# Three stages in one kernel: weights of the first expert issued together, zero stores at unit 14, a later fill tile and two tiles of tokens split early

## Chip, cores and metric

The kernel runs on one core of a Trainium2 chip. The time is device microseconds of one execution; several executions are timed and the median is given. The profile is one execution, recorded by the hardware.

## What is computed

The reference chains three stages over 1,152 tokens (2 batches of 576) of width 512, in float32.

```python
scores = scale * np.matmul(q, k.transpose(0, 1, 3, 2))      # 8 heads of 64
scores = np.where(masks, scores, -1000000000.0)             # 4 heads: last 32 keys; 4 heads: every 32nd key
x = softmax(scores) @ v                                     # -> (1152, 512)
logits = x @ w_gate + modality_bias[modality_id]            # 8 experts
e_idx = np.argmax(logits, axis=1)
out[e_idx == e] = gate_w * (np.maximum(x @ w1[e], 0) @ w2[e])   # one expert a token; w1 512x1024, w2 1024x512
# second layer: 4 experts, every token through all of them
out += p[:, e:e+1] * (np.maximum(x @ w1[e], 0) @ w2[e])
```

## The kernel before

**Attention** (first 66 us). The masked attention is cut into 20 units of 128 rows (`units`, `NU` = 20): six strided ones and five local ones for the first batch (units 0 to 10), then five strided and four local ones. A software pipeline over `s` runs `scores(s)`, `transp(s-2)`, `norm(s, s-4)`, `pv(s-3)` and `xtr(s-5)`. `norm` also stores the unit's result rows to the scratch `xe` in HBM (lines 378 and 383) from the SyncE queue (SP): one store for a local unit, two for a strided one. Every DMA of SP takes the next of eight semaphores in turn and waits until the one that had it before has landed.

**Routing and the fill tile.** The gate's logits of the first batch give the most frequent expert while the second batch is still in attention (`route0`). Up to 128 of its tokens become the *fill tile*: `first_tile` gathers their rows from `xe` (line 596), and the generator `plain_tile` (lines 609 to 653), kept as `fill`, computes them in plain float32 between other work. Its steps: one with four transposes (line 617), eight with a first-layer matmul each (line 623; the profile shows a float32 matmul as two), one with eight transposes (line 636), four with second-layer matmuls (line 643), then the scaling and the store (lines 652, 653). `early(n)` runs it up to step n; the list `EF` gives n for the last units, for the place after `logits_part(1, 0)`, after the first step of `logits(1)`, and after the rest. The expert's eight weight blocks of 512 KB go to `raws[0..7]`: two in `route0` (`W1A` = 2), the others from unit 20 on (`W1S`), two and then one for each later `s`, between the row stores of units 17 to 19. Five stores of zeros to rows of `ye` that no tile writes (line 736) are issued at `s == NU - 1`.

After the second batch's logits, `ranks` and a chain of small VectorE operations (lines 778 to 843) place every token in one of 11 tiles of 128 by expert (`idx16`). Two gathers (line 852) fetch the rows of tiles 0 and 1; the four-matmul transposes of tile 0 (line 860) stand between the fill tile's second-layer steps 12 and 13. A conditional block for more tiles (line 911) follows; it is skipped here.

**First expert layer** (`moe1`, to about 235 us). The float32 operands are split into a high part, cast by ScalarE (line 846), and a low part, subtracted by VectorE (line 847), and each product takes three matmuls. `Weights.ahead(most)` splits blocks in the order of their use while fewer than `most` are held; a block whose expert is the one of the tile before is not loaded again (a skipped DMA). `moe1` runs `mm1` of tile k (four blocks) between the transposes of the hidden rows of tile k-1 (`htr`, line 1032), then `mm2` of tile k-1 (lines 1046 to 1048). `xprep(k)` gathers the gate weights of tile k, transposes and splits its tokens (`x_parts`) and issues the gather of tile k+2. The PSUM pool `ps_a` of these transposes has two banks; a bank is free when VectorE has taken the low part from it. All engines run their own instructions in program order.

**Second expert layer** (from about 235 us) is not touched.

Of the kernel before, what the change touches and what calls it, by code (L numbers as in the profile page):

```python
# [28 lines left out]
KC = DM // P  # L29
FC = FF // P  # L30
# [81 lines left out]
def fused_kernel(  # L112
# [37 lines left out]
    RING, RAW = 10, 8  # L150
# [10 lines left out]
    def load_block(raw, src, cond=None):  # L161
        nc.sync.dma_start(out=raw.rearrange("p (c f) -> p c f", c=src.shape[1]), in_=src, cond=cond)
# [134 lines left out]
    NU = len(units)  # L297
# [88 lines left out]
    def transp(u):  # L386
        kind, i = units[u]
        w = KW if kind == 0 else GQ
        pt = ps2.tile([P, 512], F32, name="ps_t")[:, : 2 * P].rearrange("p (a b) -> p a b", a=2)
        for pr in range(2):  # L390
            nc.tensor.transpose(
                pt[: 2 * w, pr], st[u][:, 2 * pr : 2 * pr + 2].rearrange("p h k -> p (h k)"), ident
            )
        pts = a3.tile([P, 2, P], F32, name="pts")
        nc.scalar.copy(pts[: 2 * w], pt[: 2 * w])
        st[u] = pts
# [271 lines left out]
    def route0():  # L668
        logits_part(0, 1)
        logits_part(0, 0)  # L670
        yield from logits(0)
        rk = ranks(0)
        fav = favourite(rk[:, TPB])
        for _ in range(4):
            next(fav)
        eg.append(expert_value(gtab[0:1, 0:1]))
        for c in range(W1A):
            load_block(raws[c], w1_block(eg[0], c))
        yield
        for n, _ in enumerate(turns(lanes(0, rk), fav)):  # L680
            if n % 2:
                yield
        yield from first_tile()
# [20 lines left out]
            filled += 1  # L704


    W1A, W1S = 2, 20
    nw = W1A
    r0 = route0()
    EF = 0, 0, 1, 1, 1, 2, 4  # L710
    for s in range(NU + 5):
        if s == 9:
            ax.close()
            gp = ctx.enter_context(tc.tile_pool(reuse_waits="tile", name="gp", bufs=5, side="right"))
            xctx = ctx.enter_context(ExitStack())
            xp = xctx.enter_context(tc.tile_pool(reuse_waits="tile", name="xp", bufs=2, side="right"))
            ectx = ctx.enter_context(ExitStack())
            ep = ectx.enter_context(tc.tile_pool(reuse_waits="tile", name="ep", bufs=1, side="right"))
            ge = gp.tile([P, XW], F32, name="g")
            ye0 = xp.tile([P, XW], F32, name="ye0", bufs=1)  # L720
            zero = ep.tile([P, FF], F32, name="he")
            nc.gpsimd.memset(zero[:, :XW], 0.0)
        if s < NU:
            scores(s)
        if 0 <= s - 2 < NU:
            transp(s - 2)
        norm(s, s - 4)
        if 0 <= s - 3 < NU:
            pv(s - 3)
        if 0 <= s - 5 < NU:  # L730
            xtr(s - 5)
        if s == 12:
            late_setup()
        if s == NU - 1:
            for t in range(NST + 1, NSX + 1):
                nc.sync.dma_start(out=ye[t * P : (t + 1) * P, :], in_=zero[:, :XW])
        if s - 5 >= nb0 - 1:
            next(r0, None)
            if s >= R2:
                next(r0, None)  # L740
        if s == NU:
            for _ in r0:
                pass
            logits_part(1, 1)
        if s >= W1S and W1A <= nw < FC:
            for _ in range(2 if s==W1S else 1):
                load_block(raws[nw], w1_block(eg[0], nw) if nw < KC else w2_block(eg[0], nw - KC))
                nw += 1
        if s > NU:
            early(EF[s - NU - 1])  # L750
    while nw < FC:
        load_block(raws[nw], w2_block(eg[0], nw - KC))
        nw += 1
    logits_part(1, 0)
    early(EF[4])
    lg = logits(B - 1)
    next(lg)
    early(EF[5])
    for _ in lg:
        pass  # L760
    early(EF[6])
    rk = ranks(B - 1)
# [100 lines left out]
    def x_parts(g, pt=None):  # L863
        pt = pt or x_transposed(g)
        xh = xp.tile([P, 512], F32R, name="xh")
        xl = xp.tile([P, 512], F32R, name="xl")
        split(xh, xl, pt)
        return xh, xl

    gs = {k: m1_gather(k, gp) for k in range(2)}  # L870
    for n in range(5):
        if n == 3:
            x0 = x_transposed(gs[0])
# [131 lines left out]
    def moe1(mp, tiles, W, gs, pool, mid, after, before_last):  # L1005
        n = len(tiles)
        xs, hs, ys = {}, {}, {}

        def xprep(k):
            g = gs.pop(k)  # L1010
            y = mp.tile([P, XW], F32, name="y", bufs=3)
            with_rows(y, idx16[:, tiles[k] : tiles[k] + 1])
            xs[k] = x_parts(g) if k else x0
            ys[k] = y
            if k + 2 < n:
                gs[k + 2] = m1_gather(tiles[k + 2], pool)

        def mm1(k, ph, kc):
            xh, xl = xs[k]
            key = "1", tiles[k], kc  # L1020
            wh, wl = W.out.pop(key)
            s = slice(P * kc, P * (kc + 1))
            for xx, ww, first, last in ((xh, wh, kc == 0, False), (xh, wl, False, False), (xl, wh, False, kc == KC - 1)):
                for i in range(2):
                    nc.tensor.matmul(ph[i], xx[:, s], ww[:, 512 * i : 512 * (i + 1)], start=first, stop=last)  # L1025
            W.release(key)

        def htr(k, i, ht):
            pt = pst.tile([P, 512], F32, name="ps_a")
            for c in range(4):  # L1030
                s = slice(512 * i + P * c, 512 * i + P * (c + 1))
                nc.tensor.transpose(pt[:, P * c : P * (c + 1)], hs[k][:, s], ident)  # L1032
            hh = mp.tile([P, 512], F32R, name="hh")
            hl = mp.tile([P, 512], F32R, name="hl")
            split(hh, hl, pt)
            ht.append((hh, hl))

        def mm2(k, ht, py, u):
            key = "2", tiles[k], u
            wh, wl = W.out.pop(key)  # L1040
            for i in range(2):
                kc = 2 * u + i
                hh, hl = ht[kc // 4]
                s = slice(P * (kc % 4), P * (kc % 4 + 1))
                f = slice(512 * i, 512 * (i + 1))
                nc.tensor.matmul(py, hh[:, s], wh[:, f], start=(kc == 0), stop=False)  # L1046
                nc.tensor.matmul(py, hh[:, s], wl[:, f], start=False, stop=False)  # L1047
                nc.tensor.matmul(py, hl[:, s], wh[:, f], start=False, stop=(kc == FC - 1))  # L1048
            W.release(key)

        xprep(0)
        xprep(1)
        W.ahead()
        for k in range(n + 1):
            ht = []
            if k == n:
                before_last(W, 0)
            if k < n:
                ph = [psb.tile([P, 512], F32, name="ps_b") for _ in range(2)]
                mm1(k, ph, 0)  # L1060
            if k > 0:
                htr(k - 1, 0, ht)
            W.ahead()
            if k == n:
                before_last(W, 1)
            if k < n:
                mm1(k, ph, 1)
            if k > 0:
                htr(k - 1, 1, ht)
            W.ahead()  # L1070
            if k < n:
                mm1(k, ph, 2)
                if 0 < k < n - 1:
                    xprep(k + 1)
                W.ahead()
                mm1(k, ph, 3)
                h = mp.tile([P, FF], F32, name="h")
                for i in range(2):
                    nc.scalar.activation(h[:, 512 * i : 512 * (i + 1)], ph[i], AF.Relu)
                hs[k] = h  # L1080
                W.ahead()
            if k > 0:
                py = psb.tile([P, 512], F32, name="ps_b")
                for u in range(4):
                    mm2(k - 1, ht, py, u)
                    if k == n and u < 3:
                        before_last(W, 2 + u)
                    mid(tiles[k - 1], u)
                    if u < 3:
                        W.ahead()  # L1090
                y = ys.pop(k - 1)
                nc.scalar.activation(y[:, :DM], py, AF.Copy, scale=y[:, DM : DM + 1])  # L1092
                t = tiles[k - 1]
                nc.scalar.dma_start(out=ye[(t + 1) * P : (t + 2) * P, :], in_=y)
                W.ahead()
                after(t)
# [275 lines left out]
    places2 = [[(m2b[n][1], len(m1b) + n) for n in (2 * u, 2 * u + 1)] for u in range(NU2)]  # L1372
    W = Weights(m1b + m2b, raws, len(m1b))
    PC = Pieces()
    W.ahead(3)
    x0 = x_parts(gs[0], x0)
    W.ahead(4)
    for _ in fill:
        pass
    W.owner[KC:] = [None] * (RAW - KC)  # L1380
    W.load()
    W.ahead()
    ectx.close()
    x2p = ctx.enter_context(tc.tile_pool(reuse_waits="tile", name="x2p", bufs=1))
    xh2, xl2 = (x2p.tile([P, 7, 2, HP * CHT[0]], F32R, name=n) for n in ("xh2", "xl2"))
# [211 lines left out]
```

## Time and profile before

| what | value |
|---|---|
| median of 3 runs | 631.07 us (630.07 to 634.13) |
| profiled execution | 631.46 us |
| its span on the core | 629.7 us |
| mean granted TensorE clock | 0.987 |
| TensorE (PE) matmuls, busy | 596.2 us (95% of the span) |
| VectorE, ScalarE, GpSimd busy | 417.2, 350.7, 249.5 us |
| DMA | 79.14 MB, mean 126 GB/s |

Busy times of engines overlap. PEld is TensorE's weight loads, which run beside matmuls. A granted clock of 1.00 is 2.4 GHz and 0.50 is 1.2 GHz. Times in the rows are microseconds from the span's start; in a group's row the mean is in nanoseconds. An idle time in square brackets is that of the engine just before the instruction, with what ended it.

### The profile page before, as it was taken

Reading aid. Unit: us, or ns where it says so; the run is one execution under the profiler, and the core shown is the slowest. Engines: PE = TensorE matmul, PEld = TensorE weight load, DVE = VectorE, ACT = ScalarE, POOL = GpSimd, SP = SyncE. Lnnn points to the kernel's source line nnn. Section 1 sums busy time; section 2 is a strip of 40 time slices with the busy share of each in tenths; the row PEclk is TensorE's granted clock in tenths of the full one; section 3 lists DMA queues with packets and bytes.
Section 4 is the critical chain, followed back from the end, with each engine's and each line's share of the span. In section 5 each row is a group of like instructions: output and inputs, shape, how many; then the busy total and the mean of one; then the engine's idle time right before and its main releaser. Section 6 shows DMA issues by size and latency. Waiting matters only on the chain.

```text
span 629.7 us, 10388 instructions
## 1 busy us (share of the span) xinstructions
PE 596.2 (95%) x3620; PEld 498.8 (79%) x3620; DVE 417.2 (66%) x738; ACT 350.7 (56%) x690; POOL 249.5 (40%) x309
## 2 busy tenths in 40 slices
PE   4897798999999989999999999999999999999995
PEld 3554446888877878888988889898889988999984
DVE  3467369999896875668677677575565567557541
ACT  2354169888988874555656555554444544444420
POOL 9312023113696444275657656332342112312203
PEclk9999799999998999999999999999999999999999
DMA  8983951543479764353223231322421223121002
GB/s 189 200 187 109 315 161 47 168 143 94 144 229 316 231 222 150 122 165 101 101 92 110 72 129 68 135 84 88 144 87 67 69 74 124 71 68 68 0 2 84
DMA packets 35346, 79.14 MB, mean 126 GB/s; under 512 B 6520, under 2 KB 9856, under 8 KB 34904
## 3 DMA queue, kind: packets, MB, share of 16 engines
q1 hardware_dynamic: 30632, 67.08, 33.8%
q0 software_dynamic: 2784, 7.95, 4.1%
q10 hardware_dynamic: 1872, 3.39, 1.4%
q8 instruction: 30, 0.49, 0.3%
q14 instruction: 28, 0.23, 0.1%
HBM read 98.49 MB, written 9.28 MB: 171 GB/s over the span
## 4 chain that ended last, share of the span: by engine, by line
PE 77%; ACT 2%; DVE 2%; issue 2%; DMA 2%; POOL 1%; SPq 0%; POOLq 0%; DVEq 0%; ACTq 0%
PE ps_b L1269 9%; PE ps_b L1270 9%; PE ps_b L1271 9%; PE ps_b L1025 8%; PE ps_b L1418 7%; PE ps_b L1417 7%; PE ps_b L1420 7%; PE ps_a L1417 3%; PE ps_a L1418 3%; PE ps_a L1420 3%; PE ps_b L1048 3%; PE ps_b L1047 2%; PE ps_b L1046 2%; PE ps_a L1032 1%; ACT wh L846 1%
## 5 line engine op out<-in xcount | busy, mean ns | idle before, releaser
L1189 DVE TENSOR_TENSOR wl<-raw,wh 128x512 fp32r<-128x512 f32 (+1 forms) x160 | 125.6, 786 | 51.7 <-ACT wh L1188 51.0
L847 DVE TENSOR_TENSOR wl<-raw,wh 128x1024 fp32r<-128x1024 f32 x88 | 107.5, 1252 | 20.0 <-ACT wh L846 19.6
L1188 ACT CAST wh<-raw 128x512 fp32r<-128x512 f32 (+1 forms) x160 | 102.9, 664 | 3.5 <-POOL raw L1212 3.3
L1209 POOL TENSOR_TENSOR raw<-raw 128x256 f32<-128x256 f32 x32 | 24.1, 753 | 200.1 <-DVE wl L1189 200.1
L846 ACT CAST wh<-raw 128x1024 fp32r<-128x1024 f32 x88 | 90.1, 1055 | 8.6 <-ACT y L1092 3.6
L1281 DVE TENSOR_TENSOR m2t<-ps_b,raw 128x320 f32<-128x320 f32 (+1 forms) x93 | 42.1, 453 | 40.3 <-PE ps_b L1271 39.2
L1269 PE MATMUL ps_b<-xh,wh 128*128 128x256 f32 x224 | 63.8, 285 | 1.0 <-DVE xh L1281 0.5
L1271 PE MATMUL ps_b<-xh,wl 128*128 128x256 f32 x224 | 63.0, 281 | 0.0
L1270 PE MATMUL ps_b<-xl,wh 128*128 128x256 f32 x224 | 63.0, 281 | 0.0
L1269 PE MATMUL ps_b<-x,wh 128*128 128x320 f32 x160 | 49.6, 310 | 0.0
L1270 PE MATMUL ps_b<-x,wh 128*128 128x320 f32 x160 | 49.4, 309 | 0.0
L1271 PE MATMUL ps_b<-x,wl 128*128 128x320 f32 x160 | 49.4, 309 | 0.0
L1269 PEld LDWEIGHTS ps_b<-xh,wh 128*128 128x128 f32 x224 | 42.2, 189 | 7.1 <-ACT raw L1302 0.9
L1270 PEld LDWEIGHTS ps_b<-xl,wh 128*128 128x128 f32 x224 | 42.2, 188 | 4.2
L1284 ACT ACTIVATE hh2b<-m2t 128x256 fp32r<-128x256 f32 (+1 forms) x45 | 20.0, 443 | 44.3 <-DVE m2t L1281 41.0
L1284 ACT ACTIVATE hh2a<-m2t 128x256 fp32r<-128x256 f32 (+1 forms) x42 | 18.7, 445 | 44.5 <-DVE m2t L1281 44.5
L1271 PEld LDWEIGHTS ps_b<-xh,wl 128*128 128x128 f32 x224 | 42.3, 189 | 0.0
L605 POOL DMA_INDIRECT y<-xx,idx x11 | 12.9, 1177 | 60.4 <-DMA ye<-y 41.3
L1046 PE MATMUL ps_b<-wh,hh 128*128 128x512 f32 x88 | 35.1, 399 | 1.5 <-ACT hh L846 1.5
L1417 PE MATMUL ps_b<-wh,hh2a 128*128 128x512 f32 x90 | 35.5, 395 | 0.0
L1418 PE MATMUL ps_b<-wl,hh2a 128*128 128x512 f32 x90 | 35.5, 395 | 0.0
L1417 PE MATMUL ps_b<-wh,hh2b 128*128 128x512 f32 x90 | 35.5, 394 | 0.0
(274 smaller groups left out, 1546.0 us busy)
## 6 DMA issues: line engine op xcount, KB each, us to landing
raw<-in_w1a_dram SPq DMA_DIRECT2D x48, 512.0 KB
raw<-in_w2a_dram SPq DMA_DIRECT2D x48, 512.0 KB
raw<-in_w1b_dram SPq DMA_DIRECT2D x32, 512.0 KB
raw<-in_w2b_dram SPq DMA_DIRECT2D x32, 512.0 KB
ye<-y ACTq DMA_DIRECT2D x11, 260.0 KB
kvl<-in_kvl_dram SPq DMA_DIRECT2D x2, 792.0 KB
ye<-he SPq DMA_DIRECT2D x5, 260.0 KB
kvl<-in_kvl_dram SPq DMA_DIRECT2D x2, 614.0 KB
```

Of the source, the lines that this page charges most:

```text
L846: nc.scalar.copy(dst_h, src)
L847: nc.vector.tensor_tensor(dst_l, src, dst_h.bitcast(F32), op=ALU.subtract)
L1025: nc.tensor.matmul(ph[i], xx[:, s], ww[:, 512 * i : 512 * (i + 1)], start=first, stop=last)
L1046: nc.tensor.matmul(py, hh[:, s], wh[:, f], start=(kc == 0), stop=False)
L1188: return (lambda: nc.scalar.copy(h[:, s], src[:, s])), (lambda: nc.vector.tensor_tensor(l[:, s], src[:, s], h[:, s].bitcast(F32), op=ALU.s ...
L1189: lambda: nc.vector.tensor_tensor(l[:, s], src[:, s], h[:, s].bitcast(F32), op=ALU.subtract)
L1269: nc.tensor.matmul(ph, wh[:, kc], xh, start=first and kc == 0, stop=False, skip_group_check=True)
L1270: nc.tensor.matmul(ph, wh[:, kc], xl, start=False, stop=False, skip_group_check=True)
L1271: nc.tensor.matmul(ph, wl[:, kc], xh, start=False, stop=kc == 1, skip_group_check=True)
L1417: nc.tensor.matmul(po, hh, wh, start=(fb == 0 and fh == 1), stop=False, skip_group_check=part)
L1418: nc.tensor.matmul(po, hh, wl, start=False, stop=False, skip_group_check=part)
L1420: nc.tensor.matmul(po, hl, wh, start=False, stop=last, skip_group_check=part)
```

## The change

The edits are of order only; no instruction computes anything else. `W1A` becomes 1 and the other seven weight blocks are all issued at `s == 20`, ahead of the stores of units 17, 18 and 19. The zero stores move from `s == 19` to `s == 14` (`ZS`), right behind the store of unit 10. `EF` drops all of the fill tile's steps from the loop: its transposes come behind the first step of `logits(1)` instead of ahead of the last `xtr` and of `logits_part(1, 0)`, and its later steps move back by one. Before `moe1`, tile 0's tokens are split after two blocks instead of three, tile 1's tokens are transposed and split after five blocks (before: in `xprep(1)`, after ten), and nine blocks instead of ten are split ahead. In `moe1` the calls of `W.ahead` during tile 0 fall away but for the one behind its `Relu`, which then splits five blocks.

```diff
-    W1A, W1S = 2, 20
+    W1A, W1S, ZS = 1, 20, 14
...
-    EF = 0, 0, 1, 1, 1, 2, 4
+    EF = 0, 0, 0, 0, 0, 1, 3
...
-        if s == NU - 1:
+        if s == ZS:
             for t in range(NST + 1, NSX + 1):
                 nc.sync.dma_start(out=ye[t * P : (t + 1) * P, :], in_=zero[:, :XW])
...
         if s >= W1S and W1A <= nw < FC:
-            for _ in range(2 if s==W1S else 1):
+            while nw < FC:
                 load_block(raws[nw], w1_block(eg[0], nw) if nw < KC else w2_block(eg[0], nw - KC))
                 nw += 1
...
-            xs[k] = x_parts(g) if k else x0
+            xs[k] = x_parts(g) if k > 1 else x01[k]
...
         xprep(0)
         xprep(1)
-        W.ahead()
         for k in range(n + 1):
...
             if k > 0:
                 htr(k - 1, 0, ht)
-            W.ahead()
+                W.ahead()
...
             if k > 0:
                 htr(k - 1, 1, ht)
-            W.ahead()
+                W.ahead()
             if k < n:
                 mm1(k, ph, 2)
                 if 0 < k < n - 1:
                     xprep(k + 1)
-                W.ahead()
+                if k:
+                    W.ahead()
                 mm1(k, ph, 3)
...
-    W.ahead(3)
-    x0 = x_parts(gs[0], x0)
-    W.ahead(4)
+    W.ahead(2)
+    x01 = [x_parts(gs[0], x0)]
+    W.ahead(KC + 1)
+    x01.append(x_parts(gs[1]))
+    W.ahead(KC + 2)
     for _ in fill:
         pass
     W.owner[KC:] = [None] * (RAW - KC)
     W.load()
-    W.ahead()
+    W.ahead(RING - 1)
```

## Rows read from the trace of the kernel before

**Rows 1.** The page: busy time by engine, share of the span, instructions.
```profile
PE 596.2 (95%) x3620; PEld 498.8 (79%) x3620; DVE 417.2 (66%) x738; ACT 350.7 (56%) x690; POOL 249.5 (40%) x309
```

**Rows 2.** Busy time by stretch: engines, then granted clock, DMA share, GB/s.
```profile
60.00:70.00 10.00, 5.43 (x67) 3.65 (x66) 3.92 (x19) 2.19 (x7) 2.73 (x3) 0.89 0.73 237
70.00:80.00 10.00, 10.00 (x43) 4.49 (x42) 4.89 (x36) 1.42 (x4) 0.00 (x0) 0.77 0.96 335
...
90.00:100.00 10.00, 7.69 (x33) 5.50 (x32) 9.86 (x10) 9.59 (x12) 7.40 (x6) 1.00 0.28 84
...
110.00:120.00 10.00, 10.00 (x52) 8.21 (x51) 9.28 (x10) 8.73 (x12) 2.18 (x2) 1.00 0.42 131
...
80.00:81.00 1.00, 1.00 (x3) 0.29 (x2) 0.93 (x5) 0.60 (x1) 0.00 (x0) 1.00 1.08 413
```

**Rows 3.** Timeline of TensorE: start, duration, line, operation, tiles, count, idle before.
```profile
68.86 1.12 PE L617 MATMUL ps_t<-mk,g 128*128 128x128 f32 x4 [2.76 <-DMA g<-xe,idxe]
...
82.66 3.70 PE L643 MATMUL ps_a<-raw,hte 128*128 128x512 f32 x8
86.19 0.60 PE L860 MATMUL ps_a<-mk,g 128*128 128x128 f32 x4
86.63 3.60 PE L643 MATMUL ps_a<-raw,hte 128*128 128x512 f32 x8
91.53 0.66 PE L860 MATMUL ps_a<-mk,g 128*128 128x128 f32 x4 [1.30 <-DVE xl L847]
```

**Rows 4.** Timeline of the SyncE queue, issue of the zero stores and weights.
```profile
56.06 4.43 SPq L383 DMA_DIRECT2D xe<-raw  x6
...
66.20 3.93 SPq L736 DMA_DIRECT2D ye<-he  x5
70.23 0.77 SPq L378 DMA_DIRECT2D xe<-rw  x1
71.22 1.13 SPq L162 DMA_DIRECT2D raw<-in_w1a_dram  x2
...
74.79 0.42 SPq L378 DMA_DIRECT2D xe<-rw  x1
```

**Rows 5.** Line 852 from 79 to 84 us: its instructions in ns, first and last start.
```profile
L852 POOLq EVENT_SEMAPHORE  x4: 17/43/1659, 79.3 to 81.1; - x4
...
DMA to landing us min/median/max: 3.4/3.5/3.6
```

**Rows 6.** Timeline at the start of the first expert layer: ScalarE, VectorE, TensorE's next wait.
```profile
86.30 2.94 ACT L846 CAST wh<-raw 128x1024 fp32r<-128x1024 f32 x3 [3.13 <-SPq L911]
...
91.39 8.26 DVE L847 TENSOR_TENSOR wl<-raw,wh 128x1024 fp32r<-128x1024 f32 x7
...
91.67 5.79 ACT L846 CAST wh<-raw 128x1024 fp32r<-128x1024 f32 x6 [0.41 <-ACT ye L652]
...
100.69 1.08 ACT L1079 ACTIVATE h<-ps_b 128x512 f32<-128x512 f32 x2
...
104.71 0.68 DVE L847 TENSOR_TENSOR hl<-ps_a,hh 128x512 fp32r<-128x512 f32 x1
...
105.45 0.66 PE L860 MATMUL ps_a<-mk,g 128*128 128x128 f32 x4 [0.22 <-DVE hl L847]
```

**Rows 7.** The chain that ended last, pieces of TensorE: start, duration.
```profile
92.19 5.62 PE ps_b L1025 x24
...
106.11 1.39 PE ps_b L1025 x6
...
114.40 0.44 PE ps_a L1032 x4
```

**Rows 8.** TensorE after its wait at 187 us, and stretches around both waits.
```profile
189.68 0.66 PE L1136 MATMUL ps_b<-mk,g 128*128 128x128 f32 x4 [2.29 <-DMA g<-ye,cidx]
...
69.00:74.00 5.00, 5.00 (x20) 2.48 (x21) 0.00 (x0) 1.17 (x3) 0.00 (x0) 0.50 0.90 308
...
190.00:194.00 4.00, 4.00 (x14) 3.18 (x12) 1.33 (x1) 3.14 (x7) 3.36 (x7) 0.58 1.03 358
```

## The prediction

> **What bounds the kernel now.** The page comes first: TensorE is busy for 95% of the span [rows 1]. The stretches then show where it is not the bound: from 110 us on it is busy throughout, but between 60 and 70 us it works little more than half the time, and between 90 and 100 us three quarters [rows 2]. All edits lie between 56 and 106 us, so only there can time be won, and what TensorE has won when it stops waiting is kept.
>
> The timeline of TensorE names its waits [rows 3]. At 68.86 it has stood 2.76 us for the rows of the fill tile, at 91.53 it has stood 1.30 us for VectorE. In the five microseconds after the first wait the granted clock is 0.50, that is 1.2 GHz [rows 8]. The five zero stores take 3.93 us of SyncE's queue just ahead of most weight blocks [rows 4]. ScalarE starts the splits of the first expert layer at 86.30, released by SyncE after 3.13 us of waiting, and from there VectorE sets the pace: TensorE's transposes of tile 2's tokens, at 105.45, wait for its `hl` [rows 6]. The start of these transposes is where I measure the gain; TensorE's next long wait, at 187 us, is of another kind [rows 8].
>
> **The fill tile's place.** Gone is the wait of 2.76 us, and the 1.2 GHz of 69 to 74 us if TensorE keeps working: five microseconds at half rate held 2.5 us of work [rows 3, 8]. One step of two matmuls, 3.70 / 4 = 0.9 us by those of line 643 [rows 3], moves from ahead of `ranks` to behind it. That would be 6 us; I take 5 as the lead of the routing chain, since the transposes of the fill tile still stand ahead of the logits'. Behind `ranks` come six steps instead of five, 0.9 us longer, and they need weight block 1 (below), which I let cost 0.6: line 643 starts 3.5 us earlier, at 79.2, and its first half ends at 79.2 + 3.7 = 82.9.
>
> **The zero stores.** Issued behind unit 10's store, they precede the six stores that begin at 56.06. Their price on SyncE moves with them: at most the 3.93 us of before, at least 5 x 0.42 = 2.1 us, the duration of the store at 74.79 [rows 4]. I take 2.6, nearer to the lower end, as fewer transfers are queued there. Behind them wait the stores of units 11 to 13, the gate weights' store, block 0 and the stores of units 14 and 15, later by 2.6 us until block 1, no longer issued there, gives back about 0.7. None of these ends a wait: the fill tile's rows are of units 0 to 10, and block 0 has the fill tile's transposes ahead of its first use. At 66.20 their 1.3 MB are out of the way.
>
> **The weights.** Unit 16's store goes out near 68.0 in place of 70.23. Blocks 1 to 7 follow every 0.75 us from 68.6 to 73.2: between the 0.57 of the pair at 71.22 and the 0.99 from the store to it [rows 4]. For a block with nothing ahead of it I take 3.7 us to landing, a little over the 3.5 of a gather [rows 5]: block 1 is there at 72.3. The others are bound by DMA, 0.524 MB each: 1.56 us at 335 GB/s, the mean of 70 to 80 us, 1.27 at 413, the best second [rows 2]. I take 1.4, between: block 7 at 80.7. The stores of units 17 to 19 (0.39 MB, 1.1 us) are issued no earlier than before, when the last went out at 74.79 [rows 4], but behind all seven blocks instead of among them: they land at 81.8. Before, GpSimd's wait for them ended at 79.4 + 1.66 = 81.1 [rows 5]. So **the last result rows win nothing**: the gathers of tiles 0 and 1 need every row, go out at 82.0, and tile 0's rows arrive 3.4 us later [rows 5], at 85.4. SyncE's wait for all its transfers, before two blocks behind the last rows, ends two to three microseconds sooner, and ScalarE's first split moves from 86.30 to about 83.5. That lead is not the bound, because the two tiles' tokens stand early in ScalarE's order.
>
> **TensorE at the gather.** Ready at 82.9, it stands until 85.4 for tile 0's transposes, 2.5 us that were not there before. Then 86.19 to 90.23 repeats, 4.05 us [rows 3], to 89.5. Tile 1's transposes find their bank free (the 1.30 us are gone), take 0.66 us and have the branch ahead of them, for which I take 0.3: they end at M = 90.4, against 92.19 [rows 3, 7].
>
> **Splits for tiles 0 and 1.** Tile 1's tokens now stand ahead of block 5 in the orders of ScalarE and VectorE, and both wait for them until M. From there ScalarE has the token cast (0.5), block 5 at 0.965 (5.79 / 6), the fill tile's scaling and store with their wait (1.1) and blocks 6 to 8 (2.9): 5.5 us [rows 6]. The two `Relu` follow, just when the products of tile 0 have ended (5.62 us, rows 7), for 1.1 us [rows 6], and only then block 9, since the calls between the products are gone: it is cast at M + 7.6. VectorE then needs five blocks at 1.16 (8.26 / 7, less the overlap) and `hl`, 0.68 [rows 6]: M + 14.1 = 104.5. TensorE gets to tile 2's transposes after 5.62 + 3 x 1.39 + 2 x 0.44 = 10.7 us [rows 7] and stands there for **3.4 us in one piece**; before, the wait at this place was 0.22 [rows 6]. The transposes start at 104.55 in place of 105.45: 0.9 us won.
>
> **The clock.** After 2.76 us of idling it fell to 0.50, and after 2.29 us it fell too, to a mean of 0.58 over 190 to 194 us [rows 3, 8]. After 1.30 us it did not: 90 to 100 us have 1.00 [rows 2, 3]. The shorter fall costs 0.42 x 4 = 1.7 us. I charge one, for the 3.4 us, and leave the one at 82.9 open, since that idling is the difference of two estimates.
>
> **Sum.** -0.9 + 1.7 = +0.8 us. On the profiled execution, 631.46 us with 1.8 us outside its span of 629.7, that is 632.3; the median of the runs is 0.4 lower, so 631.9 us there.
>
> **Rivals.**
> - *Both waits drop the clock.* TensorE idles at 82.9 for more than about 2 us, and the second half of line 643 runs at 1.2 GHz: another 1.7 us, or 2.5 if the fall lasts like that of 69 to 74 us. For: 2.5 us of idling is more than the 2.29 that did it. Against: whatever delays the early blocks shortens it. It decides from 2 us of idling on, and gives 631.9 + 1.7 = 633.6 to 634.4, slower than before. Chance 0.25.
> - *The rows come sooner.* At 413 GB/s block 7 lands at 72.3 + 6 x 1.27 = 79.9 and the rows at 80.9: M and all behind it come 0.9 earlier and TensorE's first wait is below 2 us. If the clock then holds through the second wait too, 631.07 - 1.8 = 629.3; another microsecond from ScalarE's early start gives 628. For: five microseconds of the routing chain are gone. Against: the five splits behind the `Relu`. Chance 0.27. The Trainium skill, page "SBUF — State Buffer", section "The DMA setup-cost knee", puts a transfer at 2 us plus its bytes at 436 GB/s; by that, as an estimate, the 4.06 MB issued from 68.6 on are in at 79.9, two microseconds sooner than I have the rows, and the sum would come to 630.0. By that rule the whole wait at 82.9 is short; no stretch read here moves more than 413 GB/s.
> - *The order does nothing.* SyncE pays 3.93 us at 56 us, the blocks go out hardly sooner than at 71.22, and the gathers and the first split stay where they are: 631. Chance 0.05.
>
> **How the numbers follow.** The forecast has a chance of 0.43 and 630.0 to 633.4 as its own range: the rows' landing by the two DMA paces (about a microsecond either way), with the issue price of the zero stores (up to 1.3 late, 0.5 early) in it. The predicted time is 631.9 us. The range of 627.8 to 634.6 takes in the faster rival and the double fall. A measurement of this kernel cannot tell less than about 1%, 6.3 us, from no change. Faster by that would take the whole lead of the routing chain and more, 0.03; slower by that two long falls and late zeros, 0.03; within it 0.94.
>
> **What would show it.** Right: the wait before line 617 is gone and the clock stays at 1.00 until 80 us; the gathers of line 852 still go out near 82; tile 0's transposes wait for a DMA; tile 2's wait for `hl` more than 2 us, with 1.2 GHz behind it. Wrong: gathers before 81 us, products of tile 0 before 89 us, or a clock that holds after both waits (below 629.5); or hardly a wait for `hl`, because VectorE never stood for tile 1's tokens. A time under 627 or over 636 would mean that something outside 56 to 106 us had moved.

## The result, and the profile after

The changed kernel takes 636.06 us (median of 20 runs, 630.88 to 638.68), the kernel before, run beside it, 631.69. The ratio of the means is 1.0058, with a 95% interval of 1.0038 to 1.0079: some 3.7 us slower. The forecast was 631.9 us, with a range of 627.8 to 634.6. The interval excludes 1, so the loss is clear of noise, but it is smaller than the 1% that the prediction set as its bound for a change. The profiled execution took 637.23 us.

The page: TensorE is as busy as before [rows 1], in a span that is 5.8 us longer.

```profile
span 635.5 us, 10384 instructions
...
PE 596.9 (94%) x3620; PEld 499.5 (79%) x3620; DVE 417.3 (66%) x738; ACT 351.2 (55%) x690; POOL 249.9 (39%) x309
```

Stretches, columns as in [rows 2]:

```profile
60.00:70.00 10.00, 7.70 (x90) 4.08 (x90) 4.54 (x21) 3.23 (x11) 3.34 (x4) 0.83 0.55 174
70.00:80.00 10.00, 8.64 (x39) 4.08 (x38) 6.38 (x43) 1.74 (x4) 0.00 (x0) 1.00 0.99 348
80.00:90.00 10.00, 6.70 (x35) 3.41 (x34) 2.75 (x4) 4.50 (x7) 1.91 (x2) 0.98 0.51 147
90.00:100.00 10.00, 9.70 (x33) 6.04 (x32) 7.04 (x8) 6.95 (x9) 3.97 (x4) 0.85 0.18 51
100.00:110.00 10.00, 6.72 (x36) 5.30 (x35) 9.62 (x10) 9.50 (x13) 4.17 (x3) 1.00 0.21 61
110.00:120.00 10.00, 10.00 (x41) 8.03 (x40) 8.60 (x9) 7.78 (x10) 0.00 (x0) 0.83 0.01 5
```

Between 60 and 70 us TensorE is busy 2.3 us longer, though part of that at half clock (the mean is 0.83), and between 70 and 80 it has the full clock. Then it stands twice, in 80 to 90 and in 100 to 110 us, and the clock falls behind each wait. The timeline of TensorE names them (beside [rows 3, 6]):

```profile
70.21 0.66 PE L617 MATMUL ps_t<-mk,g 128*128 128x128 f32 x4
...
74.71 5.42 PE L623 MATMUL ps_s<-raw,xte 128*128 128x512 f32 x12 [0.87 <-DMA raw<-in_w1a_dram]
79.97 0.45 PE L842 MATMUL ps_x<-boh,aoh 96*128 96x16 f16 x12
...
81.65 3.70 PE L643 MATMUL ps_a<-raw,hte 128*128 128x512 f32 x8 [0.18 <-ACT hte L639]
88.47 0.66 PE L860 MATMUL ps_a<-mk,g 128*128 128x128 f32 x4 [3.12 <-DMA g<-xe,idx]
88.97 5.29 PE L643 MATMUL ps_a<-raw,hte 128*128 128x512 f32 x8
94.56 0.63 PE L860 MATMUL ps_a<-mk,g 128*128 128x128 f32 x4 [0.30 <-PEq L911]
...
109.15 0.66 PE L860 MATMUL ps_a<-mk,g 128*128 128x128 f32 x4 [3.28 <-DVE hl L847]
```

The wait ahead of line 617 is gone. In its place TensorE stands 3.12 us for tile 0's rows, then works through line 643 in 5.29 us instead of 3.60, and stands 3.28 us for `hl` ahead of tile 2's transposes, which start at 109.15 instead of 105.45. The stretches just behind the two waits, beside those of [rows 8]:

```profile
89.60:93.00 3.40, 3.40 (x5) 1.35 (x4) 2.96 (x3) 2.99 (x4) 0.00 (x0) 0.50 0.04 10
110.10:113.50 3.40, 3.40 (x9) 2.63 (x8) 3.40 (x5) 3.12 (x5) 0.00 (x0) 0.50 0.00 0
```

SyncE's queue, beside [rows 4]: the zeros take 2.53 us at 56.91, seven blocks stand in a row, and the last rows' stores go out at 74.22 and after.

```profile
56.91 2.53 SPq L736 DMA_DIRECT2D ye<-he  x5
...
65.61 0.36 SPq L162 DMA_DIRECT2D raw<-in_w1a_dram  x1
...
69.71 1.39 SPq L162 DMA_DIRECT2D raw<-in_w1a_dram  x3
71.60 2.52 SPq L162 DMA_DIRECT2D raw<-in_w2a_dram  x4
74.22 2.12 SPq L378 DMA_DIRECT2D xe<-rw  x3
```

Line 852, beside [rows 5], on GpSimd's queue: the last rows are seen to land at 84.0 instead of 81.1, and the gathers start at 85.0 and 86.3. The first line below is of the kernel before, the other two of the changed kernel.

```profile
L852 POOL DMA_INDIRECT g<-xe,idx x2: 952/952/953, 82.0 to 83.3; - x2
...
L852 POOLq EVENT_SEMAPHORE  x4: 17/43/43, 84.0 to 84.3; - x4
L852 POOL DMA_INDIRECT g<-xe,idx x2: 952/954/956, 85.0 to 86.3; - x2
```

ScalarE at the start of the first expert layer, beside [rows 6]. The line to compare is the first: its first split, released by SyncE, starts at 86.06, where it started at 86.30. New are the 1.12 and 2.64 us for which it stands for the tokens of tiles 0 and 1.

```profile
86.06 1.99 ACT L846 CAST wh<-raw 128x1024 fp32r<-128x1024 f32 x2 [3.96 <-SPq L911]
89.17 0.58 ACT L846 CAST xh<-ps_a 128x512 fp32r<-128x512 f32 x1 [1.12 <-PE ps_a L860]
...
95.23 0.59 ACT L846 CAST xh<-ps_a 128x512 fp32r<-128x512 f32 x1 [2.64 <-PE ps_a L860]
...
101.65 4.83 ACT L846 CAST wh<-raw 128x1024 fp32r<-128x1024 f32 x5
```

### The profile page after: what moved, and what is told of

The parts are those of the page before. It is cut to its first block, busy times and chain, and to the rows that moved or that the text cites. A ratio compares the mean times of both kernels' runs of the same rounds, so it can differ in the third digit from the quotient of the medians.

```text
span 635.5 us, 10384 instructions
## 1 busy us (share of the span) xinstructions
PE 596.9 (94%) x3620; PEld 499.5 (79%) x3620; DVE 417.3 (66%) x738; ACT 351.2 (55%) x690; POOL 249.9 (39%) x309
## 4 chain that ended last, share of the span: by engine, by line
PE 76%; ACT 2%; DMA 2%; issue 2%; DVE 2%; POOL 1%; POOLq 0%; ACTq 0%; DVEq 0%
PE ps_b L1269 9%; PE ps_b L1270 9%; PE ps_b L1271 9%; PE ps_b L1025 7%; PE ps_b L1420 7%; PE ps_b L1419 7%; PE ps_b L1422 7%; PE ps_a L1419 3%; PE ps_a L1420 3%; PE ps_a L1422 3%; PE ps_b L1048 3%; PE ps_b L1046 2%; PE ps_b L1047 2%; ACT wh L846 1%; PE ps_a L1032 1%
## 5 line engine op out<-in xcount | busy, mean ns | idle before, releaser
L1048 PE MATMUL ps_b<-wh,hl 128*128 128x512 f32 x88 | 35.4, 402 | 0.1
```

## The experiments

Ratios are to the kernel before, run beside each kernel on the same chip, with 95% intervals. `hl` is the low part of tile 0's hidden rows, split by VectorE; a fall of the clock is a stretch at a granted clock of 0.50.

**One part taken back at a time.** Each is the changed kernel with one part as before.

Weights (two blocks early, the others among the last rows):

```diff
-    W1A, W1S, ZS = 1, 20, 14
+    W1A, W1S = 2, 20
...
-        if s == ZS:
+        if s == 14:
...
-            while nw < FC:
+            for _ in range(2 if s==W1S else 1):
```

> The changed kernel with one part undone: the weight blocks go out as before the change (two early, the others between the row stores of units 17 to 19). Theory A (the late rows): in the changed kernel TensorE waits 3.12 us before tile 0's transposes, since the gathers of line 852 go out at 85.02 instead of 82.02, and the clock falls behind that wait. With the rows among the blocks again the gathers go out near 82 or before, that wait is at most 1.5 us, no 1.2 GHz follows it, and the time is 2.5 to 4 us below the changed kernel's. Rival B (the order of the splits alone): the gathers move but the time does not follow, since the wait for hl (3.28 us) stays and sets the end; 0 to 1.5 us below the changed kernel.

Measured: 1.0019 (0.9989 to 1.0049). TensorE's wait ahead of tile 0's transposes is 0.38 us, as theory A had it, but the gathers start at 83.9 and not near 82. The wait for `hl` stays, 3.62 us, with half clock behind it.

```profile
87.36 0.66 PE L860 MATMUL ps_a<-mk,g 128*128 128x128 f32 x4 [0.38 <-DMA g<-xe,idx]
...
106.77 1.12 PE L860 MATMUL ps_a<-mk,g 128*128 128x128 f32 x4 [3.62 <-DVE hl L847]
```

Of the four parts this one gives back most, but its interval overlaps that of the changed kernel and those of the next runs. The changed kernel itself, timed again (below), had 1.0039 (1.0017 to 1.0062). So the times of these four runs do not rank the parts; their traces show which wait each part brings.

Splits (tokens of tile 1 in `xprep(1)`, the calls of `W.ahead` in and ahead of `moe1` as before):

> The changed kernel with the early split of tile 1's tokens and the calls of ahead in and before the first expert layer set back to the order of before. Theory B (the order of the splits): the one wait of 3.28 us for hl falls apart into pieces of about one microsecond, the clock holds there, and the time is 2 to 4 us below the changed kernel's, although the wait of about 3 us before tile 0's transposes stays. Theory A alone (the late rows do it): the two tiles' tokens come no sooner, VectorE's backlog is the same, and the time stays within 1 us of the changed kernel's.

Measured: 1.0033 (1.0014 to 1.0052). The wait for `hl` is 0.25 us and no clock falls behind it, as theory B had it; the one for tile 0's rows is 4.01 us. The gain beside the whole change, some 1.6 us by the two ratios, lies between the two theories and is not clear of noise.

Zero stores back to unit 19, then `EF` back:

> The changed kernel with the five zero stores back at unit 19. Theory A: their 1.3 MB stand ahead of the seven blocks and of the rows behind these again, so the rows land 1 to 3 us later and the time is 0 to 3 us above the changed kernel's. Rival Z (the stores at unit 14 cost the SyncE queue 2.5 us and so delay the blocks): the blocks go out sooner and the time is 1 to 2.5 us below the changed kernel's.

> The changed kernel with the fill tile's steps back at their places of before (transposes ahead of the last unit's and of the second batch's logits). Theory A: the wait for the fill tile's rows returns (2.76 us before the change) and TensorE gets to tile 0's transposes later, but these wait for the rows of units 17 to 19 anyway, so the wait before them shrinks by what comes back ahead of it and the time stays within 1.5 us of the changed kernel's. Rival F (the new place of the fill tile costs the time, by idling TensorE later): 2 us or more below the changed kernel's.

Measured: 1.0065 (1.0045 to 1.0085) and 1.0053 (1.0034 to 1.0073). Without the early zeros TensorE stands 3.36 us for weight block 1 instead of 0.87 and the gathers start at 87.4. With `EF` back the wait for the fill tile's rows does not return, as its expectation had it; TensorE stands 2.23 us for block 1 instead. The runs do not tell either of the two from the whole change.

**Rows ahead of the blocks.**

```diff
-    W1A, W1S, ZS = 1, 20, 14
+    W1A, W1S, ZS = 1, 23, 14
```

> Changed kernel, with all seven weight blocks issued behind the stores of units 17 to 19 instead of ahead of them. Theory A (the gathers go out late because the last rows land behind seven blocks): the gathers of tiles 0 and 1 go out as soon as the routing list is there, near 81 to 82 instead of 85.0, the wait ahead of tile 0's transposes is under 1 us and the clock stays at 1.00 behind it; but block 1 is issued about 3 us later, so that the fill tile's second half waits longer for it (0.87 us before, up to 3). The time is 2 to 4 us under the changed kernel's if that wait stays under 2 us, and within 1 us of it if it drops the clock. Rival B (the rows' landing is not what the gathers wait for, but the routing list): the gathers stay at 84 to 85 and the time is that of the changed kernel or worse.

Measured: 1.0049 (1.0023 to 1.0074). Theory A fell; rival B had the place, not the reason. The timeline of TensorE and line 852 in this kernel:

```profile
76.22 7.88 PE L623 MATMUL ps_s<-raw,xte 128*128 128x512 f32 x12 [3.74 <-DMA raw<-in_w1a_dram]
83.94 0.45 PE L842 MATMUL ps_x<-boh,aoh 96*128 96x16 f16 x12
...
89.10 0.60 PE L860 MATMUL ps_a<-mk,g 128*128 128x128 f32 x4
```

```profile
L852 POOLq EVENT_SEMAPHORE  x3: 43/43/43, 75.0 to 75.2; - x3
L852 POOL DMA_INDIRECT g<-xe,idx x2: 952/952/953, 84.9 to 86.1; - x2
```

GpSimd's waits for the rows no longer hold anything at 75 us; now the routing list (the row numbers `idx` that the gathers read) is late, because its matmul (line 842) stands on TensorE behind twelve of the fill tile's that wait 3.74 us for blocks. So the gathers start at 84.9, where they started. Rows and blocks both stand ahead of the gathers; whichever goes last sets them.

> Changed kernel with the seven blocks behind the stores of units 17 to 19 and with the order of splits of the kernel before; the zero stores and the logits stay where the change put them. Theory A (late rows and the order of the splits are what the change costs, the two other edits gain): gathers near 81 to 82, waits ahead of tile 0's and tile 2's transposes under 1.5 us, no fall of the clock behind them: 629 to 631.5, as fast as the kernel before or up to 2 us faster. Rival B (the earlier logits and zeros gain nothing because block 1 is then what the fill tile waits for): 631.5 to 634.

Measured, with the splits of before besides: 1.0036 (1.0014 to 1.0059), rival B. The waits ahead of tiles 0 and 2 are gone, as theory A had it, but 2.15 us for block 1 with a fall of the clock are there.

**The calls during tile 0 put back.**

> Changed kernel, with the calls that issue weight splits between the products of tile 0 put back; the tokens of tile 1 are still split early, ahead of block 5. Theory A (five splits stand behind the Relu of tile 0 because those calls are gone, and hl of tile 2 behind them): the split of blocks 9 and on goes on beside tile 0's products, hl comes 1 to 3 us earlier, the wait ahead of tile 2's transposes falls from 3.28 to under 2 us and the clock holds: 2 to 4 us less than the changed kernel. Rival B (what delays hl is that tile 1's early tokens hold up both engines until TensorE has turned them): the wait stays near 3 us and so does the time.

Measured: 1.0058 (1.0036 to 1.0080). Theory A fell: the wait only moves, to the `Relu` that now stands behind these splits.

```profile
103.46 1.11 PE L1032 MATMUL ps_a<-mk,h 128*128 128x128 f32 x4 [2.82 <-ACT h L1078]
```

**One part alone, on the kernel before.** The zero stores and `EF` of the change; then its order of splits.

> Kernel before, with the zero stores at unit 14 and the logits ahead of the fill tile's transposes; weight blocks and splits as before. Theory A (the change loses by the rows behind seven blocks and by the splits, its two other edits gain): with the blocks among the last rows, as in the run with the weights put back, the gathers go out near 84 or sooner and the wait ahead of tile 0's transposes is under 1 us; with the splits of before the wait of 3.6 us for hl and the half clock behind it are gone, tile 2's transposes start at 104 to 105.5. 628.5 to 631, level with the kernel before or up to 2 us under it. Rival B (the earlier logits only hand the wait on to weight block 1, 2.2 us with a fall of the clock, so nothing is gained at the gathers): gathers at 83 to 84, later than the 82.0 of before, tile 2's transposes at 105.5 to 107, 631 to 633.

> Kernel before, with the new order of splits alone (both tiles' tokens early, no split calls between the products of tile 0). Theory A (the missing calls put five splits behind the Relu and hl behind them): gathers at 82.0 as before, the first expert product 0.5 to 1 us earlier than 91.9, then a wait of about 3 us for hl with half clock behind it, tile 2's transposes near 105 to 107 and 1.7 us lost to the clock: 632 to 634, 1 to 3 us slower. Rival B (the wait for hl of the changed kernel comes from its late gathers, as hl is paced from there on): the wait is under 1.5 us, the clock holds, 629.5 to 631.

Measured: 0.9997 (0.9981 to 1.0014) and 1.0021 (1.0003 to 1.0039). Zeros and logits alone are level with the kernel before: gathers at 81.4, tile 2's transposes at 104.38, as theory A had it in the trace; the time, 631.25 us, is just above its range. Their interval lies below both of the changed kernel's, so the loss comes with the two other edits, weights and splits. The splits alone make the second wait, theory A, with a granted clock of 0.50 in 107.1 to 110 us, though their gathers start at 84.2 and not at 82.0:

```profile
107.06 1.11 PE L860 MATMUL ps_a<-mk,g 128*128 128x128 f32 x4 [3.53 <-DVE hl L847]
```

**Both kernels profiled once more.**

> The kernel before, profiled once more. Theory A (the 1.2 GHz between 62 and 79 us that some kernels with the earlier logits or zeros show, for 3 to 17 us, belongs to them): again 1.00 from 60 us to the wait before the fill tile's transposes. Rival B (it differs from one execution to the next of the same kernel): a stretch of 0.50 in 62 to 68 us may stand here too.

> The changed kernel, profiled once more. Theory A (the waits of 3.1 us ahead of tile 0's transposes and 3.3 us for hl belong to the order of the work): both again, between 2.5 and 4 us, each with half clock behind it, gathers between 84 and 86. Rival B (they are of one execution): one of them under 2 us. The stretch at 0.50 from 62.3 us may be longer, shorter or absent if it differs between executions.

The changed kernel shows the same: gathers at 84.0 and 85.3, waits of 3.41 and 3.25 us, tile 2's transposes at 109.16, span 635.1. The kernel before does not; stretches, then TensorE:

```profile
60.00:70.00 10.00, 6.44 (x75) 3.52 (x67) 4.25 (x19) 2.52 (x9) 3.05 (x4) 0.77 0.63 203
...
90.00:100.00 10.00, 8.33 (x34) 5.67 (x33) 9.86 (x11) 9.59 (x12) 6.37 (x5) 1.00 0.26 71
```

```profile
87.48 0.66 PE L860 MATMUL ps_a<-mk,g 128*128 128x128 f32 x4 [0.24 <-DMA g<-xe,idx]
87.97 3.60 PE L643 MATMUL ps_a<-raw,hte 128*128 128x512 f32 x8
93.04 0.66 PE L860 MATMUL ps_a<-mk,g 128*128 128x128 f32 x4 [1.47 <-DVE xl L847]
...
106.95 0.66 PE L860 MATMUL ps_a<-mk,g 128*128 128x128 f32 x4 [0.21 <-DVE hl L847]
```

Here the clock falls at 62 us too, the gathers start at 84.0, and the span is 631.9: rival B. The execution that the prediction was built on (631.46 us) lay near the median of the runs, 631.69; this second one (633.67) is among the longer ones, and so are the two profiled executions of the changed kernel, 637.23 and 636.91 against a median of 636.06. Between the spans of the first pair lie 5.8 us, of the second 3.2; the means of the runs are 3.7 apart.

**TensorE kept busy in the waits.** The 24 turns are pure addition. The first call stands ahead of tile 0's transposes, the second ahead of `xprep(2)`.

```diff
+    def keep_busy(pt):
+        for _ in range(24):
+            nc.tensor.transpose(pt[:, :P], ident, ident)
...
+            keep_busy(ps2.tile([P, 512], F32, name="ps_t"))
...
+                if k == 1:
+                    keep_busy(psb.tile([P, 512], F32, name="ps_b"))
```

> Changed kernel, and TensorE turns the identity 24 times into a PSUM tile that nobody reads, once ahead of tile 0's transposes and once ahead of tile 2's: it works through its two waits. Nothing that is waited for is altered. Theory A (two waits of 3.1 and 3.3 us, each followed by 3.4 us at half clock, are what the change costs): tile 0's rows and hl come when they came, the clock stays at 1.00 behind both, the first expert product starts near 93.3 instead of 94.95 and tile 2's transposes near 107.5 to 109, about 1.7 to 3.4 us less than the changed kernel, 632.7 to 634.4 beside its 636.06. Rival B (VectorE and ScalarE set the pace from the gathers on, the clock takes nothing from the end): the first wait's fall is hidden by a longer wait for hl, and only the second is won, 1.7 us. Rival C (the slow clock has nothing to do with the waits): no change.

> The changed kernel itself, timed beside the next three on one chip: 635 to 637, ratio 1.004 to 1.008 to the kernel before. Its trace should show the wait of 3.1 to 3.4 us ahead of tile 0's transposes and that of 3.3 us for hl again, half clock behind each.

> Changed kernel, with the 24 idle turns of the identity ahead of tile 0's transposes alone. Theory A (each fall of the clock costs 1.7 us of the end; tile 2's transposes follow tile 1's by 14.6 us whatever the clock did before): the clock holds behind the gather's wait, tile 1's transposes come 1.7 us earlier against their gather, tile 2's with them, the wait for hl with its fall stays: 1.7 us under the changed kernel. Rival B (what the clock gives back is waited away for hl): no change, the wait for hl is 1.7 us longer.

> Changed kernel, with the idle turns ahead of tile 2's transposes alone. Theory A: the wait for hl ends when it did, the clock behind it is 1.00 instead of 0.50 for 3.4 us: 1.7 us under the changed kernel. Rival C (the falls in the records cost nothing that the runs can show, as the run with both suggests, whose median was not lower): the time of the changed kernel.

Measured: both 1.0078 (1.0050 to 1.0106); then, timed beside each other, the changed kernel itself 1.0039 (1.0017 to 1.0062), the first alone 1.0067 (1.0044 to 1.0090), the second alone 1.0043 (1.0024 to 1.0062). In the traces the clock holds behind each wait that is filled. With the first, line 643 takes 3.60 us again, tile 1's transposes come at 93.83 against 95.94 and tile 2's at 108.38 against 110.52, of which 0.5 us is an earlier gather (85.8 against 86.3). With the second, 109 to 113 us have 1.00. The runs do not follow: no kernel of the three is faster than the changed one, which is what rival C had. The profiles show some of it going elsewhere: the kernel with the first has half clock for twice as long behind its `hl` wait, and once more at 241 us, and those with both and with the second have half clock from 64 to 77 us. So what one fall costs the runs is not settled by these three. Windows of the kernel with the first alone:

```profile
108.00:114.50 6.50, 6.12 (x17) 4.96 (x18) 5.71 (x7) 4.12 (x6) 0.00 (x0) 0.50 0.00 1
...
241.00:244.00 3.00, 3.00 (x10) 2.25 (x9) 2.38 (x4) 1.18 (x2) 0.54 (x1) 0.50 0.13 18
```

**Blocks among the rows, TensorE busy ahead of tile 2.**

> Changed kernel with the weight blocks among the last rows, as before the change, and the idle turns ahead of tile 2's transposes. Theory A: the rows are no longer behind seven blocks, so the wait ahead of tile 0's transposes is under 1 us; the early split of tile 1's tokens brings tile 1's transposes up to 1 us sooner than in the kernel before, tile 2's follow 14.6 us later instead of 13.9, and the clock holds behind them: 630.5 to 632.3, level with the kernel before. Rival C (the falls cost nothing): 633 to 634, as with the weights put back alone.

Measured: 629.61 us, ratio 0.9970 (0.9952 to 0.9987), faster than either kernel and below what theory A had. Gathers at 81.9, both waits short, the clock at 1.00 behind them. It is 1.00 in 189 to 194 us too, behind a wait of 2.05 us where it fell in both kernels; in 230 to 237 us, where the first profile before shows no fall, it is 0.76.

```profile
85.45 0.66 PE L860 MATMUL ps_a<-mk,g 128*128 128x128 f32 x4 [0.34 <-DMA g<-xe,idx]
...
89.86 0.63 PE L860 MATMUL ps_a<-mk,g 128*128 128x128 f32 x4 [0.32 <-DVE xl L847]
...
101.04 2.78 PE L872 MATMUL ps_b<-mk 128*128 128x128 f32 x24
104.80 0.66 PE L860 MATMUL ps_a<-mk,g 128*128 128x128 f32 x4 [0.98 <-DVE hl L847]
```

Beside the run with the weights put back (1.0019, on another chip) only the turns differ.

**What holds the first split.** In the traces so far tile 2's transposes follow ScalarE's first split at a fixed distance, once its waits for TensorE are taken off. Two kernels take away what releases that split: they leave out the conditional block at line 911, whose condition is never true with these inputs.

```diff
-            for t in range(NST, NSX):
+            for t in range(0):
```

> Kernel before, with the conditional block for tiles beyond the eleventh left out (line 911; its condition is never true with these inputs), so that ScalarE's first split need not wait until SyncE has seen all its transfers land. Theory D (in 17 of 18 profiles tile 2's transposes start 19.1 to 19.4 us after ScalarE's first split, plus what ScalarE then stands for tokens; the first split is what order has to bring forward): the first split moves from 86.3 (87.8 in the second profile) to 82.5 to 85, ScalarE stands up to 2 us for tile 0's tokens, and tile 2's transposes come 1 to 2.5 us sooner: ratio 0.996 to 0.9985. Rival E (TensorE's own way through the fill tile and the gather sets it): the first split is earlier, tile 2's transposes and the time stay, ratio within 0.0015 of 1.

> Changed kernel, with the same block left out. Theory D: the first split is up to 3 us earlier, but what ScalarE wins there it stands for tile 0's and tile 1's tokens, which still hang on gathers at 84 to 86 and on the half clock behind them: tile 2's transposes follow tile 1's by 14.6 us as before, the wait for hl and its half clock stay, and the time is within 1 us of the changed kernel's, ratio 1.004 to 1.008. Rival E' (the changed kernel loses by the late first split): 2 us or more faster than the changed kernel, ratio under 1.003.

Measured: 0.9977 (0.9959 to 0.9995) and 1.0039 (1.0021 to 1.0058). Theory D holds for the first in its time and in the trace, where the split starts at 82.08 and tile 2's transposes at 104.50, though 0.6 us of that is an earlier start of this execution (58.75 against 59.36 at line 407, see below). For the second the trace is theory D's: tile 2's transposes are 14.6 us behind tile 1's and the wait for `hl` is 3.26 us. The time is just under D's range, and its interval does not exclude rival E'; the changed kernel was not timed beside it. ScalarE in the changed kernel without the branch stands 6.47 us for tile 0's tokens with what it won:

```profile
81.88 1.99 ACT L846 CAST wh<-raw 128x1024 fp32r<-128x1024 f32 x2
90.34 0.59 ACT L846 CAST xh<-ps_a 128x512 fp32r<-128x512 f32 x1 [6.47 <-PE ps_a L860]
...
96.24 0.59 ACT L846 CAST xh<-ps_a 128x512 fp32r<-128x512 f32 x1 [2.48 <-PE ps_a L860]
```

## Why the prediction was wrong

**What sets tile 2's transposes.** S is the start of ScalarE's first split, W what ScalarE then stands for TensorE before tile 2's transposes, T their start, all from timelines:

| kernel | gather | S | W | T | T - S - W |
|---|---|---|---|---|---|
| before | 82.0 | 86.30 | 0 | 105.45 | 19.15 |
| before, second profile | 84.0 | 87.81 | 0 | 106.95 | 19.14 |
| zeros and logits alone | 81.4 | 85.23 | 0 | 104.38 | 19.15 |
| splits alone | 84.2 | 87.98 | 0 | 107.06 | 19.08 |
| blocks among rows, busy | 81.9 | 85.73 | 0 | 104.80 | 19.07 |
| before without the branch | 82.1 | 82.08 | 1.18 + 1.91 | 104.50 | 19.33 |
| changed | 85.0 | 86.06 | 1.12 + 2.64 | 109.15 | 19.33 |
| changed, second profile | 84.0 | 85.06 | 1.57 + 3.21 | 109.16 | 19.32 |
| changed without the branch | 84.6 | 81.88 | 6.47 + 2.48 | 110.17 | 19.34 |

ScalarE and VectorE have 19.1 to 19.3 us of splits to do between the first split and tile 2, in either order. The profiles not in the table have 19.1 to 19.4 too, but for the one with the calls put back (21.7), where the `Relu` is late. In these traces only an earlier split or fewer waits bring tile 2 forward. S hangs on SyncE, which waits at line 911 for all its transfers. In the times of the traces it hardly moves: 86.30 and 87.81 before, 86.06, 85.06 and 87.31 in three profiles of the changed kernel.

These times need a correction, for the executions already differ ahead of the change. In the first profile of the changed kernel TensorE is 0.66 us late at line 323, before the zero stores go out at 56.91, and 0.67 us late at line 407. Before, then changed:

```profile
55.83 0.64 PE L323 MATMUL ps_s<-kvl,ql 128*32 128x128 f32 x16
59.36 0.65 PE L407 MATMUL ps_a<-kvl,pts 128*32 128x130 f32 x16 [0.27 <-ACT ro L374]
...
56.49 0.65 PE L323 MATMUL ps_s<-kvl,ql 128*32 128x128 f32 x16
60.03 0.65 PE L407 MATMUL ps_a<-kvl,pts 128*32 128x130 f32 x16 [0.27 <-ACT ro L374]
```

Over all 20 profiles this group of line 407 starts between 58.75 and 60.74, with no pattern by edit (on average at 59.70 in the 14 profiles named next and at 59.73 in the 4). Counted from it, S comes 0.9 us sooner in the first profiles and 2.6 in the second. Among the 18 profiles that keep the branch it is on average 26.6 us behind that point in the 14 with the early zero stores (25.5 to 27.4) and 27.9 in the 4 without (26.9 to 28.8). So the first split does come sooner, by about 1.3 us. Tile 2 does not get it: the rows land last now, and ScalarE stands for the tokens.

**By the prediction's own steps.**
- *The fill tile's place*: right in kind. The wait before line 617 is gone and 70 to 80 us have the full clock. The lead is smaller than the 3.5 us taken for line 643: it starts at 81.65 against 82.66, where 79.2 was forecast (80.35 against 83.53 in the second profiles).
- *The zero stores*: 2.53 us measured, 2.6 taken.
- *The weights* are **the first part of what failed**: "they land at 81.8" and "go out at 82.0". Block 1 was to land 3.7 us after its issue; it was issued at 69.71 and released TensorE at 74.71, 5.0 us. The rows landed at 84.0: block 1 went out 1.1 us later than forecast, 0.7 of it already there in the attention, and from its issue to the rows it took 14.3 us instead of 13.2. From the rows to the first gather took 1.0 us; the prediction left 0.2 for it, although the kernel before took 0.9 there (81.1 to 82.0). So 82.0 became 85.0. The last rows do not only win nothing; they lose.
- *ScalarE's first split* was to come at 83.5, two to three microseconds sooner. It came at 86.06, 0.9 us sooner by the correction above (2.6 in the second profiles). It is 1.0 us behind the first gather instead of 4.3, mostly because the gathers are later.
- *TensorE at the gather*: a wait of 2.5 us was forecast, 3.12 measured (3.41 and 3.90 in two more profiles of the same kernel).
- *Splits*: a wait for `hl` of 3.4 us "in one piece" was forecast; 3.28, 3.25 and 3.25 were measured, 14.6 us behind tile 1's transposes. The mechanism was right, and so was its length, 14.0 us from M to tile 2's transposes where 14.1 were forecast. The point it was counted from, M = 90.4, came at 95.2 (94.56 + 0.63).
- *The clock* is **the second part of what failed**: "I charge one, for the 3.4 us, and leave the one at 82.9 open". Both waits dropped it, in all three profiles of the changed kernel. The first fall keeps line 643 at 5.3 to 5.9 us instead of 3.6. ScalarE then stands 2.6 to 3.2 us for tile 1's tokens, against 1.2 at most in the kernels with this order of splits in which that clock held, and T moves with it.

Put together in the prediction's terms: tile 0's transposes start at 88.47 instead of 85.4, 3.1 us late by the rows; from there to M takes 6.7 us instead of 5.0, another 1.7 by the fall that was not charged (2.1 and 2.7 in the second profile); so T is 109.15 instead of 104.55, and the 0.9 us won became 3.7 lost. The fall that was charged came as forecast.

In place of the sum -0.9 + 1.7, by the table and for the first profiles: S -0.24, W +3.76, the 19.15 become 19.33, together +3.7 at tile 2's transposes; 3.4 us at half clock behind them, +1.7; and at line 1136 TensorE stands 2.63 us instead of 2.29 [rows 8], +0.3. That is 5.7 of the 5.8 us between the spans, of which 0.7 was there ahead of the change. For the second profiles: -2.75 + 4.78 + 0.18 + 1.7 - 0.1 = 3.8, against 3.2 us between the spans.

**The rivals.** "Both waits drop the clock" is what happened, with a chance of 0.25 and a price of 633.6 to 634.4; it lacked the late rows and so was too low as well. Its limit of 2 us was a choice between two waits: with `EF` put back TensorE stood 2.46 us there and the clock held. "The rows come sooner" is out, and with it the estimate of 630.0 from the Trainium skill's page "SBUF — State Buffer", section "The DMA setup-cost knee": by it the transfers issued from 68.6 on would be in at 79.9, or at 81.0 from the issue at 69.71, where the trace has the last of them at 84.0. "The order does nothing" is out too: the zeros cost SyncE 2.53 us and not 3.93, and the gathers did not stay where they were.

What stays open is what a single fall of the clock costs the runs. Three kernels that took one or both away were not faster; one was, by about 3 us against the run without the turns, which was timed on another chip. So 1.7 us for each fall is shown in single traces and not by the runs.

## What to carry to other kernels

Look for the engine whose work between two fixed points is constant, and measure a change by when that work may start and what it stands for; a shorter wait on TensorE is not a gain if the engine behind it gets its inputs no sooner. Before comparing times of two traces, check that they agree ahead of the change. Among transfers that share a queue and are all waited for, reordering moves the delay from one consumer to another: put last what is used last, and count who stands for it. And where the estimate of a new wait is within half a microsecond of one that dropped the clock in the same trace, charge the fall.

## What was not expected of the hardware

- The granted clock is 0.56 to 0.74 over 61 to 67 us in 16 of the 20 profiles, both kernels among them, although TensorE had stood for no longer than 0.91 us at a time from 56 us on; up to 65 us that holds for the other four as well. In three kernels it was 0.50 all through 64 to 77 us. The two profiles of the kernel before differ by 2.2 us of span, with a fall at 62 us in one of them only.
- How long TensorE stands does not alone say whether its clock falls: with `EF` put back it stood 2.46 us ahead of tile 0's transposes and the clock stayed at 1.00; with the zeros and logits alone it stood 2.19 us ahead of line 1136 and the clock fell. With the splits put back it stood 2.50 us at line 1136 and the clock stayed at 1.00.
- The seven blocks and three row stores issued from 69.71 on (4.06 MB) were in at 84.0, 284 GB/s over that stretch, while all DMA together moved 348 GB/s in 70 to 80 us.
